# Loading the second weight matrix: plain transfers in SyncE's queue and casts on chip, in place of casting transfers that GpSimd issues

## The chip, the cores and the metric

The kernel runs on one core of a Trainium2 chip. A core has a matrix engine (TensorE, PE), three engines for elementwise work (VectorE or DVE, ScalarE or ACT, GpSimd or POOL) and a sequencer without arithmetic (SyncE, SP). Each runs its own list of instructions in order and waits for the others by semaphores. TensorE reads from the on-chip memory and writes to eight accumulator banks of 128 x 512 float32 values. Transfers between the chip's memory and the core run on 16 DMA engines; an instruction on SP, ACT or POOL issues them.

The metric is the device time of one execution in microseconds, as the median of several runs. Less is better.

## What is computed

A linear attention with decay, followed by a two-layer network with the SiLU function. The attention runs over 4 batches, 8 heads, 768 positions and 64 channels in blocks; its output, 3072 tokens of 512 channels, is the input of the network.

```
# attention, per block of positions (lam: one decay per head)
intra = (qb @ kb^T * Dmask) @ vb
inter = (qb * lam_pow) @ kv_state
out[block] = intra + inter
kv_state = lam_block * kv_state + (kb * rev_pow)^T @ vb

# network on x = attention output as (3072, 512)
h = x @ w_in                       # w_in (512, 2048)
g = h * (1 / (1 + exp(-h)))
y = g @ w_out                      # w_out (2048, 512), y (3072, 512) float32
```

All inputs are float32 in memory. The kernel multiplies in bfloat16 and accumulates in float32.

## The kernel before, in words

**Tiling.** A unit is 128 tokens, and there are 24 of them. Two units make a pair, with its own loads of k, q and v, so there are 12 pairs, numbered from 0; the fifth pair is pair 4. For each pair the kernel casts k and q to bfloat16 (`cast`), scales v by the decay (`scale`), transposes k and q, and multiplies on TensorE. Pairs 0 to 3 are transposed on TensorE, the later ones by a DMA transpose (`dma_turn`, issued by SP). From pair 3 on, the state, score and output matmuls of a pair and of its predecessor are put together as a *burst* (L569 to L622); the masks, state updates and the evacuation into `xt` follow on VectorE, with some of the `xf` updates on GpSimd.

**The network.** `product1` (matmuls at L878, called P1 below) multiplies `xt` by `w_in_bf`: 16 slices of 128 columns of the hidden layer, 4 matmuls each, for two units at a time (256 columns) or four (512). ScalarE applies SiLU and writes the tiles `g`. `product2` (matmuls at L913, called P2) multiplies `g` by `w_out_bf`: 16 matmuls of 512 columns for each unit, one for each slice `ko` of w_out. The result is copied out of the bank (`osb`) and stored by a DMA that ScalarE issues.

**The order.** The program is written as tasks with dependencies, keys and an estimate of their cost on each engine that may run them. A planner (`Planner.order`) runs through them once when the kernel is built, picks at each moment the ready task with the lowest key, and so fixes the order of each engine's instructions and which engine takes a task that several may run. Buffers come from pools with fixed counts: 11 buffers of 512 KB for loads (`raw`), 8 accumulator banks, 36 tiles `g`. Since the order is fixed, a task that is late holds up everything behind it on its engine. The estimates decide the order alone; at run time the semaphores do.

**Loads.** The order of loads follows from a list of words: `u3v` is the v of pair 3, `i0` the first quarter of w_in, `o0` the first quarter of w_out. Loads of q, k, v and w_in are plain transfers in SP's queue. w_in arrives as float32, half a quarter (128 x 2 x 512) in a `raw` buffer, and its 16 pieces of 128 x 512 are cast on GpSimd, ScalarE or VectorE (`copy`, L338 to L342). w_out has another way: four transfers that GpSimd issues write bfloat16 directly into `w_out_bf`, the cast being done by the transfer. They stand behind a *gate*, a copy of one column on GpSimd (L352) that waits for the k of pair 3.

```
sequence = "u0 u1 i0 i1 u2k i2 u2q u2v i3 u3v u3k g3k o0 u3q o1 o2 o3".split()
```

In SP's queue nothing of w_out appears, so the k, q and v of pair 4 follow directly on the q of pair 3. A P2 matmul of slice `ko` waits for quarter `ko // 4` of w_out.

Of the kernel before, what the change touches and what calls it, by code (L numbers as in the profile page):

```python
# [8 lines left out]
F32 = mybir.dt.float32  # L9
# [25 lines left out]
WIDE, CAST, LARGE, PLAIN, TURN = (512, 24.0, 27.0), (256, 14.0, 31.0), (2048, 92.0, 92.0), (2048, 84.0, 84.0), (1024, 46.0, 46.0)  # L35


class Planner:
# [18 lines left out]
    def add(self, key, on, fn, deps=(), bufs=(), nbytes=0, kind=None, prior=(), late=0.0, tag=None):  # L57
        key = key if isinstance(key, tuple) else (key,)
        key = (key[0] + self.SHIFT.get(tag, 0.0),) + key[1:]
        if tag in self.HOME:  # L60
            on = {self.HOME[tag]: on[self.HOME[tag]]}
        t = Task(key, on, fn, deps, list(bufs), nbytes, kind, prior, late)
        t.tag = tag
        for b in t.bufs:
            b.left += 1
            b.pe += "PE" in t.on
        self.tasks.append(t)
        return t
# [163 lines left out]
def kernel(  # L232
# [10 lines left out]
    nc = tc.nc  # L243
# [11 lines left out]
    TIED, SOLO, CROSSED = 3, (3,), range(4, 12)  # L255
    AWAY, XAWAY, OWN = (), (), (0, 1)
    SMALL = (0, 1)
    WKEY, WCAST, WON = -2.0, {"POOL": 0.75, "ACT": 0.62, "DVE": 0.45}, [("POOL", "ACT", "DVE")] * 2 + [("POOL", "DVE"), ("POOL", "ACT")]
    FIRST_ONES, ONES_UNTIL = 10, 19.0

    ctx.enter_context(tc.manual_schedule())
    const = ctx.enter_context(tc.tile_pool(name="const", bufs=1))
# [6 lines left out]
    add = plan.add  # L269
# [4 lines left out]
    def psum_of(b):  # L274
        i = PSUM[b.pool] + b.slot
        return banks[:, i] if b.pool == "bank" else banks[:, i:i + 2]

    def tile_of(b, shape, dt, name):
        if b.tile is None:
            b.tile = psum_of(b) if b.pool in PSUM else sb.tile(shape, dt, tag=f"{b.pool}{b.slot}", name=name)  # L280
        return b.tile
# [3 lines left out]
        out=lam_sb,  # L285
        in_=bass.AP(tensor=lam.tensor, offset=lam.offset, ap=[[0, 128]] + list(lam.ap)),
# [9 lines left out]
        out=ident, in_=ident, compare_op=AL.not_equal, fill=1.0,  # L296
# [10 lines left out]
    for r in halves:  # L307
        nc.gpsimd.affine_select(
            out=tri[r], in_=tri[r], compare_op=AL.is_ge, fill=0.0,
# [22 lines left out]
    w_out_bf = const.tile([128, KO, DM], BF16, name="w_out_bf")  # L332
    w_in_r = moe_w_in.rearrange("(ko p) f -> p ko f", p=128)
    w_out_r = moe_w_out.rearrange("(ko p) f -> p ko f", p=128)

    def copy(e, o, i):
        if e == "ACT":
            nc.scalar.activation(o, i, AF.Copy)  # L338
        elif e == "DVE":
            nc.vector.tensor_copy(o, i)  # L340
        else:
            nc.gpsimd.tensor_copy(o, i)  # L342
# [2 lines left out]
        (nc.vector if e == "DVE" else nc.gpsimd).tensor_tensor(o, a, b, op=AL.mult)  # L345


    gate = const.tile([128, 32], F32, name="gate")

    def gated(key, load, i, tile):  # L350

        t = add(key, {"POOL": 0.15}, lambda e: nc.gpsimd.tensor_copy(gate[:, i:i + 1], tile()), deps=[load],  # L352
                prior=pool_last[-1:])
        pool_last.append(t)

    pool_last = []

    def pool_load(key, w, fn, bufs, nbytes, kind, late=0.0):
        t = add(key, {"POOL": w}, fn, bufs=bufs, nbytes=nbytes, kind=kind, prior=pool_last[-1:], late=late)
        pool_last.append(t)  # L360
        return t

    raw = {}
    LATE, TLATE = 4.0, 4.0

    def parts_of(n):
        return [(0, 1), (2, 3)] if n in FINE else [(0, 1, 2, 3)]
# [21 lines left out]
    wload = {}  # L389

    def load_w(key, what, j):
        if what == "o":
            def go(e):
                nc.gpsimd.dma_start(out=w_out_bf[:, 4 * j:4 * j + 4, :], in_=w_out_r[:, 4 * j:4 * j + 4, :])  # L394

            wload[what, j] = [pool_load((key, 0), 0.8, go, [], 1.0486, LARGE, 0.5)]
            return
        cs = slice(512 * j, 512 * j + 512)
        for h in range(KI // 2):
            b = Buf("raw")  # L400

            def half(e, b=b, h=h):
                nc.sync.dma_start(out=tile_of(b, [128, 2, 512], F32, "raw_w"), in_=w_in_r[:, 2 * h:2 * h + 2, cs])  # L403

            t = add((key, 0, h), {"SP": 0.55}, half, bufs=[b], nbytes=0.5243, kind=PLAIN, late=0.3,
                    tag=("load w", j, h))
            for ko in (2 * h, 2 * h + 1):
                wload[what, j, ko] = add((WKEY + j, ko), {e: WCAST[e] for e in WON[j]},
                                         lambda e, b=b, ko=ko: copy(e, w_in_bf[:, ko, cs], b.tile[:, ko % 2]), deps=[t], bufs=[b],
                                         tag=("cast w", j, ko))  # L410

    sequence = "u0 u1 i0 i1 u2k i2 u2q u2v i3 u3v u3k g3k o0 u3q o1 o2 o3".split() 
    sequence += [f"u{n}" for n in range(NU // 2) if f"u{n}" not in sequence and f"u{n}v" not in sequence]
    for n, x in enumerate(sequence):
        if x[0] == "u":
            which = ["kqv".index(x[-1])] if x[-1] in "kqv" else range(3)
            load_pair(n - 100, int(x[1:].rstrip("kqv")), which)
        elif x[0] == "g":  # L420
            j, i = int(x[1:-1]), "kqv".index(x[-1].lower())
            _, bufs, loads = raw[j]
            g = 0 if x[-1].isupper() else len(parts_of(j)) - 1
            gated((n - 100, -1), loads[i, g], n, lambda buf=bufs[i, g]: buf.tile[:, 0, 0:1])
        else:
            load_w(n - 100, x[0], int(x[1:]))

# [45 lines left out]
    def duo_tile(i):  # L473
        return tile_of(duo_of[i][0], None, F32, "xd")
# [206 lines left out]
    def attention(n):  # L681
# [34 lines left out]
        parts = parts_of(n)  # L716
        xes = [Buf("xs" if n + c in SMALL or n + c in CROSSED else "xe") for c in range(1 if final else 2)]
        xfs = [Buf("xf") for _ in range(0 if final else 2)]
# [89 lines left out]
        for g in range(2):  # L808
# [6 lines left out]
            def inter(e, i=i, g=g, used=used, box=box_x):  # L815
                t = duo_tile(i)
                if n in SMALL:

# [16 lines left out]
            def outputs(e, i=i, g=g, st=st, box=box_x):  # L835
                t = duo_tile(i)
                follow(i)
                for m in range(2):
                    for r in range(2):
# [6 lines left out]
            hold = mask_of[i]  # L846
            im = add((s + g + 0.3, 0, 0), {"PE": 0.056 * 2 * len(used)}, inter, kind="tiled" if n in SMALL else None, bufs=[buf_x, kqT] + [x[0] for _, x in used],
                     deps=hold + cv + turned[min(g, len(turned) - 1)] + [t for _, x in used for t in x[1]], tag=("inter", n, g))
            om = add((s + g + 0.3, 0, 1), {"PE": 0.43 if n in SMALL else 0.28}, outputs, deps=hold + cv + [im], bufs=[buf_x, vd, st], kind="tiled", tag=("outputs", n, g))
            outs[i] = [om]  # L850
# [51 lines left out]
    def product2(u):  # L902
        gi, gp = group_of[u]
        final = u == NU - 1
        cols = [slice(0, 256), slice(256, 512)] if final else [slice(0, 512)]
        for ci, cs in enumerate(cols):
            bank, two = Buf("bank"), Buf("two")
            w = cs.stop - cs.start
            osb = Buf("osb" if w == DM else "osh")

            def mm(e, ko, bank=bank, cs=cs, w=w):
                g, j, _ = gs[gi, ko]
                nc.tensor.matmul(psum_of(bank)[:, :w], lhsT=g.tile[:, j, 128 * gp:128 * gp + 128], rhs=w_out_bf[:, ko, cs],  # L913
                                 start=(ko == 0), stop=(ko == KO - 1))

            prev = None
            s = 4.0 + u + ci * 0.5
            for ko in range(KO):
                g, j, ta = gs[gi, ko]
                prev = add((s + ko / 16, 2), {"PE": w / 2400 + 0.0025}, lambda e, ko=ko, f=mm: f(e, ko),  # L920
                           deps=[ta, prev] + wload["o", ko // 4], bufs=[bank, g, two], kind="p2")

            def evac(e, bank=bank, osb=osb, w=w):
                copy(e, tile_of(osb, [128, w], F32, "osb"), psum_of(bank)[:, :w])

            te = add((s - 1.0, 6), {"DVE": 0.15 + w / 960, "ACT": 0.17 + w / 1200}, evac, deps=[prev], bufs=[bank, osb, two])

            def store(e, cs=cs, osb=osb):
                nc.scalar.dma_start(out=out[128 * u:128 * u + 128, cs], in_=osb.tile)

            add((s - 0.9, 7), {"ACT": 0.1}, store, deps=[te], bufs=[osb], nbytes=0.262 * w / 512, kind=LARGE)

    for n in range(NU // 2):
# [3 lines left out]
                deps=[lam_x] + ready_of[1][3][0], tag="table")  # L937
# [5 lines left out]
    for u in range(NU):  # L943
        product2(u)
# [30 lines left out]
    for start, _, e, t in planned:  # L975
        if e == "PE":
            if not at:
                occupy(vacant(0.5, start), FIRST_ONES, 512)
            elif start < ONES_UNTIL and start - at > 0.15:
                b = vacant(at, start)  # L980
# [34 lines left out]
```

## Time and profile before

| | |
|---|---|
| median of three runs | 212.11 us |
| the runs | 214.0, 212.1, 212.11 us |
| the profiled execution | 213.39 us |
| its span, first to last instruction | 211.7 us |
| granted TensorE clock | 0.998 |
| bytes read and written | 27.27 MB read, 6.29 MB written |

The busy time of the engines and the rate of the transfers, by stretches of the span:

| stretch, us | PE | DVE | ACT | POOL | GB/s moved |
|---|---|---|---|---|---|
| 20 to 30 | 9.91 | 7.87 | 7.69 | 3.51 | 355 |
| 30 to 40 | 10.00 | 7.31 | 7.80 | 3.92 | 249 |
| 40 to 50 | 9.81 | 7.29 | 7.02 | 0.61 | 217 |
| 50 to 60 | 9.09 | 1.56 | 5.24 | 0.00 | 206 |
| 60 to 70 | 9.95 | 6.09 | 6.01 | 2.37 | 338 |

TensorE's busy time counts overlapping matmuls as one stretch, and the modelled end of a matmul lies behind the start of the next. A row such as "x26" with a start and a length is a run of equal matmuls; the pace is read from the starts of the rows that follow each other. A few matmul records are missing from the trace (572 and 383 rows where 576 and 400 were issued).

The four casting transfers are issued from 33.8 to 36.9 us. The k and q of pair 5, issued by SP at 35.35 and 36.82, land 19.7 us later; the loads ahead of them took 6 to 9 us.

### The profile page before, as it was taken

Reading aid. Unit: us, or ns where it says so; the run is one execution under the profiler, and the core shown is the slowest. Engines: PE = TensorE matmul, PEld = TensorE weight load, DVE = VectorE, ACT = ScalarE, POOL = GpSimd, SP = SyncE. Lnnn points to the kernel's source line nnn. Section 1 sums busy time; section 2 is a strip of 40 time slices with the busy share of each in tenths; the row PEclk is TensorE's granted clock in tenths of the full one; section 3 lists DMA queues with packets and bytes.
Section 4 is the critical chain, followed back from the end, with each engine's and each line's share of the span. In section 5 each row is a group of like instructions: output and inputs, shape, how many; then the busy total and the mean of one; then the engine's idle time right before and its main releaser. Section 6 shows DMA issues by size and latency. Waiting matters only on the chain.

```text
span 211.7 us, 5407 instructions
## 1 busy us (share of the span) xinstructions
PE 202.5 (96%) x2343; PEld 122.6 (58%) x2364; DVE 104.5 (49%) x181; ACT 113.6 (54%) x166; POOL 22.7 (11%) x38
## 2 busy tenths in 40 slices
PE   7998999998999999999999999999999999999993
PEld 2776878865656567676864545454444444444452
DVE  3897878672038758595859696645201110111000
ACT  3687877782566457765756452735444444444121
POOL 4027426010002100010400001300000000000000
PEclk9999999999999999999999999999999999999999
DMA  4999999999999999999999340101011101110212
GB/s 118 336 379 366 365 327 286 188 217 234 184 303 333 320 266 291 123 315 226 254 266 225 92 130 0 54 3 50 0 53 50 50 0 50 53 50 0 99 53 95
DMA packets 62183, 36.00 MB, mean 170 GB/s; under 512 B 18000, under 2 KB 57168, under 8 KB 62160
## 3 DMA queue, kind: packets, MB, share of 16 engines
q1 hardware_dynamic: 56304, 27.27, 51.2%
q10 hardware_dynamic: 3744, 6.30, 8.1%
q0 software_dynamic: 2112, 2.10, 6.0%
q8 instruction: 18, 0.29, 0.6%
q14 instruction: 5, 0.04, 0.1%
HBM read 27.27 MB, written 6.29 MB: 159 GB/s over the span
## 4 chain that ended last, share of the span: by engine, by line
PE 70%; DMA 15%; SPq 7%; DVE 3%; issue 2%; POOL 1%; ACT 0%; DVEq 0%
PE banks L913 35%; PE banks L878 28%; DMA w_out_bf<-in_moe_w_out_dram 8%; SPq L378 4%; DMA raw<-in_k_dram 4%; DMA raw_w<-in_moe_w_in_dram 4%; SPq L403 3%; PE banks L578 2%; PE banks L622 2%; PE banks L585 1%; DVE st L345 1%; PE banks L611 1%; POOL w_out_bf L394 1%; DVE xs_all L345 1%; DVE kq L340 1%
## 5 line engine op out<-in xcount | busy, mean ns | idle before, releaser
L878 PE MATMUL banks<-xt,w_in_bf 128*128 128x256 bf16 (+1 forms) x572 | 113.3, 308 | 0.7 <-POOL w_in_bf L342 0.5
L913 PE MATMUL banks<-w_out_bf,g 128*128 128x512 bf16 (+1 forms) x383 | 107.1, 370 | 2.7 <-issue 1.3
L894 ACT ACTIVATE g<-banks 128x512 bf16<-128x512 f32 x96 | 70.3, 744 | 55.7 <-PE banks L878 51.7
L878 PEld LDWEIGHTS <-w_in_bf 128*128 128x128 bf16 x576 | 55.3, 98 | 30.3 <-POOL w_in_bf L342 0.9
L913 PEld LDWEIGHTS <-g 128*128 128x128 bf16 x400 | 38.5, 98 | 41.7 <-issue 1.0
L345 DVE TENSOR_TENSOR st<-banks,tri 128x512 bf16<-128x512 f32 (+1 forms) x42 | 29.6, 759 | 6.1 <-PE banks L622 5.0
L340 DVE COPY osb<-banks 128x512 f32<-128x512 f32 x8 | 5.5, 692 | 49.8 <-PE banks L913 49.8
L345 DVE TENSOR_TENSOR xt<-banks,lam_xe 128x512 bf16<-128x512 f32 x24 | 15.7, 687 | 24.1 <-PE banks L578 23.2
L338 ACT ACTIVATE osb<-banks 128x512 f32<-128x512 f32 (+1 forms) x17 | 9.7, 570 | 28.7 <-PE banks L913 28.7
L338 ACT ACTIVATE kq<-raw 64x512 bf16<-64x512 f32 (+2 forms) x29 | 22.7, 812 | 3.5 <-ACT osb L338 1.7
L345 POOL TENSOR_TENSOR xf<-y,lam_be 128x256 f32<-128x256 f32 (+1 forms) x13 | 11.9, 914 | 104.0 <-DVE y L740 104.0
L345 DVE TENSOR_TENSOR vd<-raw,lam_v 128x1024 bf16<-128x1024 f32 (+1 forms) x13 | 14.8, 1138 | 2.9 <-DMA raw<-in_v_dram 2.8
L340 DVE CAST kq<-raw 64x512 bf16<-64x512 f32 (+3 forms) x29 | 14.1, 518 | 3.3 <-DMA raw<-in_k_dram 2.5
L950 PE MATMUL banks<-ones 128*128 128x128 bf16 (+1 forms) x88 | 10.3, 266 | 1.5 <-DVE ones L291 1.5
L345 DVE TENSOR_TENSOR xs_all<-y,lam_be 64x256 bf16<-64x256 f32 (+2 forms) x21 | 9.6, 460 | 0.4
L622 PE MATMUL banks<-kqT 64*64 64x128 bf16 x288 | 9.5, 217 | 0.0
L950 PEld LDWEIGHTS <-ones 128*128 128x128 bf16 x88 | 5.9, 103 | 4.0 <-issue 2.2
L622 PEld LDWEIGHTS <-kqT 64*64 64x64 bf16 x288 | 7.4, 107 | 0.0
L740 DVE TENSOR_TENSOR y<-banks,xf 128x256 f32<-128x256 f32 (+1 forms) x17 | 6.7, 401 | 1.0 <-POOL xf L345 1.0
L611 PE MATMUL banks<-vd,kq 64*64 64x64 bf16 x240 | 6.9, 194 | 0.0
L338 ACT ACTIVATE kqT<-banks 128x512 bf16<-128x512 bf16 (+1 forms) x6 | 4.9, 810 | 2.4 <-PE banks L530 2.4
L342 POOL CAST w_in_bf<-raw_w 128x512 bf16<-128x512 f32 x8 | 5.5, 684 | 6.2 <-DMA raw_w<-in_moe_w_in_dram 6.1
(49 smaller groups left out, 73.3 us busy)
## 6 DMA issues: line engine op xcount, KB each, us to landing
out_dram<-osb ACTq DMA_DIRECT2D x23, 256.0 KB, 2.0
raw<-in_k_dram SPq DMA_DIRECT2D x11, 512.0 KB, 6.1
raw<-in_q_dram SPq DMA_DIRECT2D x11, 512.0 KB, 6.3
raw<-in_v_dram SPq DMA_DIRECT2D x11, 512.0 KB, 7.4
raw_w<-in_moe_w_in_dram SPq DMA_DIRECT2D x8, 512.0 KB, 7.9
w_out_bf<-in_moe_w_out_dram POOLq DMA_DIRECT2D x4, 512.0 KB, 14.0
raw<-in_k_dram SPq DMA_DIRECT2D x2, 256.0 KB, 4.8
raw<-in_q_dram SPq DMA_DIRECT2D x2, 256.0 KB, 5.3
```

What stands on the lines that cost most here:

```text
L338: nc.scalar.activation(o, i, AF.Copy)
L340: nc.vector.tensor_copy(o, i)
L345: (nc.vector if e == "DVE" else nc.gpsimd).tensor_tensor(o, a, b, op=AL.mult)
L378: nc.sync.dma_start(out=tile_of(bufs[i, g], [128, 2 * len(ms), 128], F32, "raw"), in_=src[i][heads(ms)].rearrange("h (p r) d -> p h (r d)" ...
L403: nc.sync.dma_start(out=tile_of(b, [128, 2, 512], F32, "raw_w"), in_=w_in_r[:, 2 * h:2 * h + 2, cs])
L611: mm = nc.tensor.matmul(psum_of(db)[d, 256 * c + 64 * k:256 * c + 64 * k + 64], lhsT=kq_of()[halves[c], 0, r, 2 * k + (h ^ c if n in CROSS ...
L622: nc.tensor.matmul(t[c, k % 2, r, :], lhsT=t_of()[halves[row], 0, r, k, c], rhs=t_of()[halves[row], 1, :, k, c], start=(k % 2 == 0 and r = ...
L740: nc.vector.tensor_tensor(tile_of(src, [128, NP, 64], F32, "y")[:, sl], d_of(), old[0].tile[:, sl], op=AL.add)
L878: nc.tensor.matmul(t[:, j, :], lhsT=w_in_bf[:, ko, 128 * m:128 * m + 128], rhs=xt[gi].tile[:, ko, :], start=(ko == 0), stop=(ko == KI - 1))
L894: nc.scalar.activation(t, psum_of(bank).rearrange("p (jc r a) -> p jc r a", r=2, a=64), AF.Silu)
L913: nc.tensor.matmul(psum_of(bank)[:, :w], lhsT=g.tile[:, j, 128 * gp:128 * gp + 128], rhs=w_out_bf[:, ko, cs], start=(ko == 0), stop=(ko == ...
L950: nc.tensor.matmul((t if b.pool == "bank" else t[:, 0])[:, 0:w], lhsT=ones[:, 0:128], rhs=ones[:, 0:w], start=True, stop=True)
```

## The change

- The four casting transfers, the gate and the chain that keeps GpSimd's issues in order are gone.
- `load_w` treats w_out as w_in: each quarter comes in two halves of 128 x 2 x 512 float32, plain transfers in SP's queue into `raw` buffers, and each half gives two pieces of 128 x 512 that are cast into `w_out_bf`. Any of GpSimd, ScalarE and VectorE may take a piece. The casts have the key `OKEY + 0.5 * j`.
- In the list of loads, two quarters (four halves) follow the q of pair 3, then come the k, q and v of pair 4, then the other two quarters.
- A P2 matmul of slice `ko` waits for the cast of piece `ko` alone.

The same bytes are read from memory. The planner is unchanged but gets other tasks, so the order of instructions changes on all engines from the q of pair 3 on.

```diff
+    OKEY = 0.0
...
-    gate = const.tile([128, 32], F32, name="gate")
-
-    def gated(key, load, i, tile):
-
-        t = add(key, {"POOL": 0.15}, lambda e: nc.gpsimd.tensor_copy(gate[:, i:i + 1], tile()), deps=[load],
-                prior=pool_last[-1:])
-        pool_last.append(t)
-
-    pool_last = []
-
-    def pool_load(key, w, fn, bufs, nbytes, kind, late=0.0):
-        t = add(key, {"POOL": w}, fn, bufs=bufs, nbytes=nbytes, kind=kind, prior=pool_last[-1:], late=late)
-        pool_last.append(t)
-        return t
...
     def load_w(key, what, j):
-        if what == "o":
-            def go(e):
-                nc.gpsimd.dma_start(out=w_out_bf[:, 4 * j:4 * j + 4, :], in_=w_out_r[:, 4 * j:4 * j + 4, :])
-
-            wload[what, j] = [pool_load((key, 0), 0.8, go, [], 1.0486, LARGE, 0.5)]
-            return
         cs = slice(512 * j, 512 * j + 512)
         for h in range(KI // 2):
             b = Buf("raw")
 
             def half(e, b=b, h=h):
-                nc.sync.dma_start(out=tile_of(b, [128, 2, 512], F32, "raw_w"), in_=w_in_r[:, 2 * h:2 * h + 2, cs])
+                nc.sync.dma_start(out=tile_of(b, [128, 2, 512], F32, "raw_w"), in_=w_in_r[:, 2 * h:2 * h + 2, cs] if what == "i"
+                                  else w_out_r[:, 4 * j + 2 * h:4 * j + 2 * h + 2, :])
 
             t = add((key, 0, h), {"SP": 0.55}, half, bufs=[b], nbytes=0.5243, kind=PLAIN, late=0.3,
-                    tag=("load w", j, h))
+                    tag=("load w" if what == "i" else "load o", j, h))
             for ko in (2 * h, 2 * h + 1):
+                if what == "o":
+                    wload[what, 4 * j + ko] = add((OKEY + 0.5 * j, ko), WCAST,
+                                                  lambda e, b=b, ko=ko: copy(e, w_out_bf[:, 4 * j + ko, :], b.tile[:, ko % 2]), deps=[t],
+                                                  bufs=[b], tag=("cast o", j, ko))
+                    continue
...
-    sequence = "u0 u1 i0 i1 u2k i2 u2q u2v i3 u3v u3k g3k o0 u3q o1 o2 o3".split() 
+    sequence = "u0 u1 i0 i1 u2k i2 u2q u2v i3 u3v u3k u3q o0 o1 u4 o2 o3".split() 
...
-                           deps=[ta, prev] + wload["o", ko // 4], bufs=[bank, g, two], kind="p2")
+                           deps=[ta, prev, wload["o", ko]], bufs=[bank, g, two], kind="p2")
```

More of the change, by code (lines that the diff above doesn't have):

```diff
@@ L419 @@
             load_pair(n - 100, int(x[1:].rstrip("kqv")), which)
[L420 to L424, printed above, removed]
         else:
```

## The prediction

> **What bounds the kernel now.** I read the page, then the chain of waits in order of time, the timelines of the engines around w_out, and the durations of the casts that w_in already gets on chip. First the page: busy time and share of the 211.7 us span by engine, and the chain's shares.
>
> ```profile
> PE 202.5 (96%) x2343; PEld 122.6 (58%) x2364; DVE 104.5 (49%) x181; ACT 113.6 (54%) x166; POOL 22.7 (11%) x38
> ...
> PE 70%; DMA 15%; SPq 7%; DVE 3%; issue 2%; POOL 1%; ACT 0%; DVEq 0%
> ```
>
> TensorE (PE) is the bound; there is little idle time to win. Where it waits, the chain in order of time (start, length) tells:
>
> ```profile
> 33.63 0.19 POOL gate L352
> 33.81 1.62 POOL w_out_bf L394 x2
> 35.44 16.02 DMA w_out_bf<-in_moe_w_out_dram
> 51.46 0.04 issue
> 51.50 0.81 PE banks L913 x3
> ```
>
> The casting transfers of w_out end a wait of PE at 51.50; behind it the chain is almost all PE to the end. PE's timeline shows the wait's size:
>
> ```profile
> 37.15 1.91 PE L878 MATMUL banks<-xt,w_in_bf 128*128 128x256 bf16 x16
> ...
> 39.96 3.01 PE L878 MATMUL banks<-xt,w_in_bf 128*128 128x256 bf16 x26
> 43.06 1.90 PE L913 MATMUL banks<-w_out_bf,g 128*128 128x512 bf16 x7
> ...
> 48.52 2.13 PE L878 MATMUL banks<-xt,w_in_bf 128*128 128x256 bf16 x18
> 51.50 0.81 PE L913 MATMUL banks<-w_out_bf,g 128*128 128x512 bf16 x3 [0.86 <-DMA w_out_bf<-in_moe_w_out_dram]
> ```
>
> A first-product matmul (P1, L878, 256 columns) takes 0.108 us in a full stretch (29 in 3.17 us from 78.27), a second-product one (P2, L913, 512 columns) 0.216 (12 in 2.59 from 70.31). So 18 P1 from 48.52 end at 50.46 and the next P2 comes 1.04 later. And 26 P1 from 39.96 end at 42.77, yet the first P2 comes at 43.06, 0.29 later. That fits the first quarter of w_out: the first issue is at 33.75, and the shortest landing is 9.3 us:
>
> ```profile
> DMA to landing us min/median/max: 9.3/14.0/18.7
> ```
>
> w_out thus costs PE about 1.04 + 0.29 = 1.3 us, and that is the whole prize: after it PE has no wait worth naming.
>
> **The change, part by part.** *Removed:* the gate and four issues on GpSimd (0.19 and 3.18 us). GpSimd is then idle for 6.5 us: worth nothing by themselves.
>
> *Added casts.* Sixteen pieces of 128x512: the built order gives GpSimd 6, ScalarE 5, VectorE 5. The same casts of w_in are in the trace:
>
> ```profile
> L342 POOL CAST w_in_bf<-raw_w x8: 611/650/822, 16.4 to 30.6; 128x512 bf16<-128x512 f32 x8
> L338 ACT ACTIVATE w_in_bf<-raw_w x6: 611/631/631, 15.9 to 30.5; 128x512 bf16<-128x512 f32 x6
> L340 DVE CAST w_in_bf<-raw_w x2: 417/628/839, 24.0 to 24.3; 128x512 bf16<-128x512 f32 x2
> ```
>
> GpSimd 6 x 0.65 = 3.9 us, ScalarE 5 x 0.63 = 3.2, VectorE 5 x 0.42 to 0.84 = 2.1 to 4.2. Cover between 36 and 54 us: GpSimd is idle but for one 0.61 us multiply at 43.39; ScalarE waits 1.21 + 0.60 + 1.86 + 2.23 = 5.9 us for PE; VectorE waits 1.72 + 0.81 + 1.83 us and then sits idle from 50.2 to 58.6. The busy time is hidden; what counts is when each piece is ready.
>
> *When the pieces land.* SP's order becomes: third input of pair 3 (q), four halves of w_out, k, q, v of pair 4, four halves, pair 5. The anchor is that q, which lands as ScalarE's cast of it starts; the pace of halves shows in GpSimd's timeline, where two casts each start on a landing, 1.42 us apart:
>
> ```profile
> 35.23 1.06 ACT L338 ACTIVATE kq<-raw 128x1024 bf16<-128x1024 f32 x1 [0.40 <-DMA raw<-in_q_dram]
> ```
> ```profile
> 18.45 0.68 POOL L342 CAST w_in_bf<-raw_w 128x512 bf16<-128x512 f32 x1 [0.61 <-DMA raw_w<-in_moe_w_in_dram]
> 19.10 0.61 POOL L345 TENSOR_TENSOR xf<-y,lam_be 128x256 f32<-128x256 f32 x1
> 19.87 0.61 POOL L342 CAST w_in_bf<-raw_w 128x512 bf16<-128x512 f32 x1 [0.15 <-DMA raw_w<-in_moe_w_in_dram]
> ```
>
> Loads of q, k, v come 1.6 us apart (k of pair 3 at 33.57, q at 35.2). So halves 0 to 3 land at 36.6, 38.0, 39.4, 40.8; pair 4 at 42.4, 44.0, 45.6; halves 4 to 7 at 47.0, 48.4, 49.8, 51.2. No buffer holds SP up: the eleven input buffers that these loads take are freed by casts done by 36.3.
>
> *When PE asks for them.* The built order is the same up to the row at 37.15, of which 10 of 16 P1 stay: end 38.23. Then 6 P2; pieces 2 and 3 (half 1: 38.0 + 0.65 = 38.7) are asked for at 38.9. Six P2 end at 39.5; the burst of pair 3 (0.97 us, from 38.99 in the trace) ends at 40.5; 24 P1 and 9 P2 with it end at 45.0; the next burst (0.96: 44.80 to 45.76) ends at E = 46.0. Then one P2 and 18 P1: piece 8 is asked for at E + 2.15 = 48.2, and half 4 plus a cast is 47.7. Piece 10 at E + 3.45 = 49.5 (half 5: 49.1), piece 12 at E + 4.75 = 50.8 (50.5), piece 14 at E + 6.36 = 52.4 (half 7: 51.9). All are in time, by 0.2 to 0.5 us.
>
> *Queues passed.* VectorE runs in order, and pieces 8, 10 and 12 stand between its xt work (1.3 us after the burst) and pair 4's casts (0.76 us each): ends at E + 1.8, E + 3.0, E + 4.2 with casts of 0.42; E + 2.2, E + 3.9, E + 5.5 with 0.84. Against E + 2.15, 3.45, 4.75 that is a wait of 0 or of 0.75; I take 0.2, nearer to the short one, since GpSimd's casts rarely run at that moment. On ScalarE the pieces stand before silus of P1 still in one of several banks: nothing.
>
> *Moved loads.* Pair 4's k and q come 5.6 us later; its transpose waits for VectorE's last cast of it, E + 3.8 = 49.8 (46.20 now). Behind pair 5's k and q (52.8, 54.4) it lands at 56.3 by the 1.9 us between the landings of q and transpose now (56.52, 58.41), or 62.0 by the longest landing, 12.2 us. Its burst comes 87 P1 and 39 P2 after E: 46.0 + 17.8 = 63.8. Covered by 2 to 7 us. Later bursts come 2.2 us earlier to 2.7 later in the order, and the least lead of a transpose now is 4 us (issued at 81.41, landed 12.0 later, for the burst at 97.36).
>
> *Sum:* -1.3 + 0.2 = -1.1 us. The profiled run is 213.39 us (span 211.7 and 1.69 around it), so 212.3; the median of the three runs is 212.11, 1.28 below it, so **211.0**.
>
> [...] The trace's VectorE casts took 417 and 839 ns, the long one beside a GpSimd cast that took 0.80. [...]
>
> **The rivals.**
> *No gain (chance 0.22): 212.1, within 0.5.* The transfers are at their limit anyway: from 35.2 to 51.5 three loads and eight halves' worth of w_out land, 11 x 0.524 MB in 16.3 us, 354 GB/s; I have the same eleven landing by 51.2. Only the order of landing against PE's order makes a gain, and slacks of 0.2 to 0.5 us can be lost: a wait at piece 2, 8 or 14 of about 1 us takes the old one's place. Against it: the last half is asked for at 52.4 where now the wait ends at 51.5 with 10 more P2 still to come before piece 15. [...]
> *Slower (0.20): the pace.* If the eleven transfers land p us apart, half 7 is cast at 35.2 + 11p + 0.65, against 52.4. My pace is 1.45; a wait begins at p = 1.51, and slower by 1% (2.1 us net) at 1.82. At p = 1.9: 56.75, 4.35 late, less 1.3: +3.1, 215.2. For it: k and q of pair 5 landed 19.7 us after issue, and the moved bytes fell to 217 GB/s from 40 to 50 us. Against: both sat beside the casting transfers; ahead of them the pace was 1.4 to 1.6.
> *Faster by over 1% (0.05).* It needs 2.1 us; PE has 1.3, and the rest would have to come out of the 1.69 us around the span, if a queue of GpSimd's is set up there. Bounds 0 and 1.69 (209.1); no row shows any of it, so 0.
>
> **Numbers.** Forecast 0.53. A measurement here tells about 1% from no change: 210.0 to 214.2. The forecast and the first rival lie within: 0.53 + 0.22 = 0.75 same; 0.20 slower by the pace, 0.05 faster. PE's order after the wait held without idle time in the trace, which is why the forecast has the most; slacks this small, why it has no more. Range 210.2 (whole prize, some of the surround) to 214.8 (p near 1.87).
>
> **What would show it.** Right: no wait of PE on w_out at 51.5, the first L913 near 38.2, the transpose of pair 4 landing before 62, PE's busy share up half a point. Wrong: a new wait ahead of L913 between 38 and 53 released by a cast (my slack was lost) or with GpSimd's casts waiting for raw_w landings over 1.8 us apart (the pace).

## The result and the profile after

| | before | after |
|---|---|---|
| median of six runs each, us | 212.12 | 215.54 |
| lowest to highest, us | 212.1 to 214.0 | 215.17 to 215.7 |
| the profiled execution, us | 213.39 | 215.7 |
| its span, us | 211.7 | 213.7 |
| round the span (time less span), us | 1.69 | 2.0 |

The kernel became slower: the ratio is 1.0137, with an interval of 1.0103 to 1.0172, so less than 2% but clear of the noise. The forecast was 211.0, with a range that ended at 214.8. Against before, +3.42 us came where -1.1 was forecast.

The page of the kernel after: span, busy time of the engines, and the shares of the chain of waits.

```profile
span 213.7 us, 5445 instructions
...
PE 204.7 (96%) x2364; PEld 122.5 (57%) x2364; DVE 109.8 (51%) x188; ACT 115.5 (54%) x169; POOL 22.6 (11%) x39
...
PE 75%; DMA 12%; SPq 8%; DVE 2%; ACT 1%; issue 1%; POOL 1%
```

TensorE's share is the same 96%, and the chain still has 20% of transfers and their issue (22% before). The shares do not say where 3.4 us went. TensorE's timeline does. Up to the loads of w_out the order of the instructions is the same on TensorE, yet the first P1 of the program starts a microsecond later; the first transfer of w_out is issued only after 32 us. First before, then after:

```profile
17.20 2.07 PE L878 MATMUL banks<-xt,w_in_bf 128*128 128x256 bf16 x15 [0.45 <-POOL w_in_bf L342]
```
```profile
18.20 0.61 PE L858 MATMUL banks<-xt,w_in_bf 128*128 128x256 bf16 x4
19.56 1.37 PE L858 MATMUL banks<-xt,w_in_bf 128*128 128x256 bf16 x11 [0.74 <-DVE st L346]
```

Going back further, VectorE's first casts wait for the first loads. In brackets stand the idle time and what ended it. Before, the first q of the program has landed at 6.01 us; after, the cast of it starts at 6.39, and a later one waits again at 9.04.

```profile
6.01 0.43 DVE L340 CAST kq<-raw 128x512 bf16<-128x512 f32 x1 [0.30 <-DMA raw<-in_q_dram]
```
```profile
6.39 0.43 DVE L341 CAST kq<-raw 128x512 bf16<-128x512 f32 x1 [0.45 <-DMA raw<-in_q_dram]
...
9.04 0.43 DVE L341 CAST kq<-raw 128x512 bf16<-128x512 f32 x1 [0.21 <-DMA raw<-in_q_dram]
```

So the same transfers, issued by the same instructions, move more slowly. The window from 5 to 15 us shows it (start:end, length, busy us of PE, PEld, DVE, ACT and POOL with counts, granted clock, DMA share, GB/s). Before, then after: 352 GB/s against 304, at the same clock of 1.00 and at a DMA share that is no lower. The DMA engines are as occupied, and move less.

```profile
5.00:15.00 10.00, 9.42 (x196) 7.29 (x198) 8.46 (x18) 7.23 (x15) 0.29 (x1) 1.00 1.11 352
```
```profile
5.00:15.00 10.00, 8.21 (x176) 6.42 (x175) 7.52 (x15) 6.19 (x14) 0.00 (x0) 1.00 1.15 304
```

The lateness grows up to the end of w_out's loads. The q of pair 3, put at 35.2 by the forecast, ends ScalarE's wait at 37.49:

```profile
37.49 1.06 ACT L339 ACTIVATE kq<-raw 128x1024 bf16<-128x1024 f32 x1 [0.20 <-DMA raw<-in_q_dram]
```

TensorE after, around w_out. The first P2 is at 40.69 (forecast 38.23). The old wait at 51.5 is gone: the P2 at 51.03 names none. New ones have come, 0.16 us ahead of piece 2 and 0.54 us at the last half:

```profile
40.69 0.81 PE L893 MATMUL banks<-w_out_bf,g 128*128 128x512 bf16 x3
41.66 0.81 PE L893 MATMUL banks<-w_out_bf,g 128*128 128x512 bf16 x3 [0.16 <-POOL w_out_bf L343]
...
51.03 1.03 PE L893 MATMUL banks<-w_out_bf,g 128*128 128x512 bf16 x4
...
56.08 1.02 PE L893 MATMUL banks<-w_out_bf,g 128*128 128x512 bf16 x4 [0.54 <-POOL w_out_bf L343]
```

The chain of waits of the kernel after (start, length, what ran) says the same: the last half of w_out lands at 46.83 + 8.54 = 55.37, GpSimd casts it, and TensorE goes on.

```profile
46.83 8.54 DMA raw_w<-in_moe_w_out_dram
55.42 0.62 POOL w_out_bf L343
56.08 1.02 PE banks L893 x4
```

From the landing of the q at 37.46 to 55.37 eleven transfers landed, on average 1.63 us apart. The forecast had 1.45. The pace is not even: the first ten are 1.53 apart, and the last half comes 2.57 behind the one ahead of it, at 52.80. The waits for casts of w_out are 0.70 us together; most of the 3.4 us was lost ahead of them.

What slows a transfer whose instruction is unchanged? One deleted line of the diff reaches every buffer: `gate`, a tile of 128 x 32 float32, takes 128 bytes of each partition of the on-chip memory and lay ahead of the load buffers. In the built program before, the first load buffer starts at byte 60672 of a partition, which is 237 x 256. After, it starts at 60544, which is 128 over a multiple of 256. All load buffers move with it, and with them every tile that is allocated behind `gate`. Single packets fit that. A load of q, k or v writes packets of 512 bytes, one of w_in packets of 2 KB; their times are read from the packet records of the two traces:

```
                     512-byte packets issued 5 to 14 us, ns     2 KB packets, 12 to 30 us, ns
                     5% / median / 95% / mean                   median / mean
before               27 / 27 / 27 / 27.2                        84 / 88.1
after                27 / 32 / 38 / 31.7                        87 / 91.0
```

### The profile page after: what moved, and what is told of

It reads as the page before. It is cut to its first block, busy times and chain, and to the rows that moved or that the text cites. A ratio compares the mean times of both kernels' runs of the same rounds, so it can differ in the third digit from the quotient of the medians.

```text
span 213.7 us, 5445 instructions
## 1 busy us (share of the span) xinstructions
PE 204.7 (96%) x2364; PEld 122.5 (57%) x2364; DVE 109.8 (51%) x188; ACT 115.5 (54%) x169; POOL 22.6 (11%) x39
## 3 DMA queue, kind: packets, MB, share of 16 engines
q1 hardware_dynamic: 58480, 31.46, 58.2%
## 4 chain that ended last, share of the span: by engine, by line
PE 75%; DMA 12%; SPq 8%; DVE 2%; ACT 1%; issue 1%; POOL 1%
PE banks L893 37%; PE banks L858 31%; DMA raw_w<-in_moe_w_out_dram 7%; DMA raw<-in_q_dram 5%; SPq L364 4%; SPq L383 4%; PE banks L602 2%; PE banks L558 2%; PE banks L565 1%; DVE st L346 1%; PE banks L591 1%; POOL w_out_bf L343 1%; ACT g L874 0%; DVE kq L341 0%; PE banks L510 0%
## 5 line engine op out<-in xcount | busy, mean ns | idle before, releaser
L858 PE MATMUL banks<-xt,w_in_bf 128*128 128x256 bf16 (+1 forms) x576 | 116.1, 308 | 0.9 <-DVE st L346 0.7
L893 PE MATMUL banks<-w_out_bf,g 128*128 128x512 bf16 (+1 forms) x400 | 113.3, 371 | 0.7 <-POOL w_out_bf L343 0.7
L341 DVE COPY osb<-banks 128x512 f32<-128x512 f32 x13 | 9.0, 692 | 57.0 <-PE banks L893 51.7
L339 ACT ACTIVATE kq<-raw 64x512 bf16<-64x512 f32 (+2 forms) x32 | 24.0, 780 | 4.1 <-DMA raw<-in_k_dram 1.7
L346 POOL TENSOR_TENSOR xf<-y,lam_be 128x256 f32<-128x256 f32 (+1 forms) x13 | 11.0, 848 | 89.3 <-DVE y L720 89.3
L341 DVE CAST kq<-raw 64x512 bf16<-64x512 f32 (+3 forms) x26 | 13.4, 534 | 5.6 <-DMA raw<-in_k_dram 2.7
L339 ACT ACTIVATE osb<-banks 128x512 f32<-128x512 f32 (+1 forms) x12 | 6.7, 561 | 16.5 <-PE banks L893 16.5
L930 PE MATMUL banks<-ones 128*128 128x128 bf16 (+1 forms) x88 | 9.7, 259 | 1.5 <-DVE ones L292 1.5
L346 DVE TENSOR_TENSOR xs_all<-y,lam_be 64x256 bf16<-64x256 f32 (+2 forms) x21 | 10.4, 497 | 0.4
L510 PE MATMUL banks<-ident,kq 128*128 128x128 bf16 x64 | 5.3, 220 | 1.9 <-DVE kq L341 1.4
```

The lines of the kernel that those rows point to most:

```text
L858: nc.tensor.matmul(t[:, j, :], lhsT=w_in_bf[:, ko, 128 * m:128 * m + 128], rhs=xt[gi].tile[:, ko, :], start=(ko == 0), stop=(ko == KI - 1))
L930: nc.tensor.matmul((t if b.pool == "bank" else t[:, 0])[:, 0:w], lhsT=ones[:, 0:128], rhs=ones[:, 0:w], start=True, stop=True)
```

## The experiments

The main theory was that the new address of the load buffers costs the time. Its rivals were the new transfers and casts themselves, and, for the part outside the span, that GpSimd no longer issues a transfer. They ran in three series, each beside before: its median was 212.51 us for the first four rows, 212.5 for the next four and 212.35 for the last. In every row, "address" is what the start of the load buffers is over a multiple of 256 bytes. The ratio, with its 95% interval, is not the quotient of the two medians.

| kernel | address | median, us | runs | ratio to before, interval |
|---|---|---|---|---|
| after_pad128 | 0 | 212.81 | 10 | 1.0016, 0.9989 to 1.0043 |
| after_pad256 | 128 | 215.85 | 4 | 1.0157, 1.0133 to 1.0182 |
| before_shift128 | 128 | 215.86 | 4 | 1.016, 1.0137 to 1.0184 |
| before_wout256 | 0 | 212.33 | 10 | 0.9985, 0.9965 to 1.0005 |
| after_loads_only | 0 | 212.71 | 10 | 1.003, 1.0 to 1.0061 |
| after_pad64 | 192 | 215.66 | 4 | 1.0163, 1.0137 to 1.0189 |
| after_pad384 | 0 | 213.04 | 10 | 1.0028, 1.0009 to 1.0046 |
| after_pad128_pool | 0 | 213.14 | 10 | 1.0025, 1.0002 to 1.0048 |
| before_without_wout | 0 | 212.21 | 12 | 0.9989, 0.996 to 1.0018 |

With the address given back the changed kernel is equal to before or slightly slower: the four intervals reach from 0.9989 to 1.0061, and for after_pad384 and after_pad128_pool they lie just above 1.

### The 128 bytes given back, and twice as many

The kernel after with an unused tile where `gate` was. For after_pad256 it is 64 wide.

```diff
+    pad = const.tile([128, 32], F32, name="pad")
     raw = {}
```

> The changed kernel with an unused tile of 128 bytes per partition where the gate tile stood; nothing else differs, so every load buffer has its address of before again (a multiple of 256 bytes; in the changed kernel 128 over). Theory A, the addresses: the loss sits in the first 30 us, where both kernels issue the same loads and the changed one lands them later; with the old addresses the 512-byte packets take 27 ns again, the first P1 starts near 17.2 us and the time is about 211.0 to 212 us (the prediction's sum). Rival B, the queue: the loss comes with the absence of GpSimd's DMA queue or with the casts, and addresses do not matter: 215.5 us again, first P1 near 18.2.

> The changed kernel with an unused tile of 256 bytes per partition: an added tile, but the load buffers stay 128 bytes off a multiple of 256. Theory A: 215.5 us, as the changed kernel. If any shift or any added tile helped, it would fall to 212. Rival B: 215.5.

An unused tile takes the loss away, and a larger one brings it back: 215.85 - 212.81 = 3.04 us, with the same instructions in both kernels. The page of after_pad128: its span, the DMA queue of the loads (packets, MB, share of 16 engines' time; 58.2% in the kernel after for the same packets and bytes), and the chain, in which transfers have 7% instead of 12.

```profile
span 210.5 us, 5422 instructions
...
q1 hardware_dynamic: 58480, 31.46, 53.5%
...
PE 86%; DMA 7%; ACT 2%; issue 2%; DVE 1%; POOL 1%; SPq 0%
```

The window from 5 to 15 us of after_pad128 moves 341 GB/s, near the 352 of before:

```profile
5.00:15.00 10.00, 9.71 (x192) 7.62 (x194) 8.37 (x18) 7.20 (x15) 0.23 (x1) 1.00 1.10 341
```

TensorE of after_pad128. Against the same rows of after (18.20, 40.69, 56.08) it is ahead by 0.95, then 2.19, then 3.16 us, and it names a wait on w_out only once, 0.23 us:

```profile
17.25 2.03 PE L859 MATMUL banks<-xt,w_in_bf 128*128 128x256 bf16 x15 [0.44 <-POOL w_in_bf L343]
...
38.50 0.60 PE L894 MATMUL banks<-w_out_bf,g 128*128 128x512 bf16 x2
39.32 0.81 PE L894 MATMUL banks<-w_out_bf,g 128*128 128x512 bf16 x3 [0.23 <-POOL w_out_bf L343]
...
52.92 1.03 PE L894 MATMUL banks<-w_out_bf,g 128*128 128x512 bf16 x4
```

### The same shift in the kernel before

before_shift128 has only a wider `gate`. before_wout256 has that, and a tile of 128 bytes ahead of `w_out_bf`, which lies 128 over a multiple of 256 in both kernels: with both edits `w_out_bf` and the load buffers start on multiples of 256. Both kernels have this edit:

```diff
-    gate = const.tile([128, 32], F32, name="gate")
+    gate = const.tile([128, 64], F32, name="gate")
```

And before_wout256 alone:

```diff
+    pad = const.tile([128, 32], F32, name="pad")
     w_out_bf = const.tile(
```

> The kernel before with a gate tile of 256 bytes per partition in place of 128: all transfers as before, the load buffers 128 bytes off a multiple of 256. Theory A: the first P1 starts near 18.2 us and the time goes up by 2 to 4 us, to 214 to 216. Rival B: 212.1.

> The kernel before with the tile that the casting transfers write, w_out_bf, moved to a multiple of 256 bytes (it lies 128 over in both kernels); the load buffers keep their alignment. Theory A in its wide form, any transfer is slowed by such an address: the casting transfers land earlier than 51.5 us and the 1.0 us wait for them shrinks, time 211.2 to 212. In its narrow form, only 512-byte packets are slowed, and rival B: 212.1.

Without any of the change's transfers or casts, the shift alone costs 215.86 - 212.51 = 3.35 us. In its trace the casting transfers start later too, and TensorE waits 1.22 us for the first quarter of w_out; how much of the 3.35 us this makes is not shown. TensorE's first P1 in before_shift128 starts where it does after, at 18.21:

```profile
18.21 0.61 PE L878 MATMUL banks<-xt,w_in_bf 128*128 128x256 bf16 x4 [0.21 <-POOL w_in_bf L342]
```

The address of `w_out_bf`, which the casting transfers write, made no difference that shows: 0.9985, and the interval holds 1.

### Loads alone, and other distances

In after_loads_only the load buffers have a pool of their own behind 128 bytes; the other tiles stay 128 bytes over a multiple of 256, as they are after, though most of them move. after_pad64 and after_pad384 are after_pad128 with a pad of 16 and of 96 columns.

```diff
+    ld = ctx.enter_context(tc.tile_pool(name="ld", bufs=1))
...
-            b.tile = psum_of(b) if b.pool in PSUM else sb.tile(shape, dt, tag=f"{b.pool}{b.slot}", name=name)
+            b.tile = psum_of(b) if b.pool in PSUM else (ld if b.pool in ("raw", "rawh") else sb).tile(shape, dt, tag=f"{b.pool}{b.slot}", name=name)
...
+    pad = ld.tile([128, 32], F32, name="pad")
```

> The changed kernel with its load buffers in a region of their own that begins with an unused 128-byte tile: the load buffers lie at multiples of 256 bytes, all other buffers (bfloat16 copies, transposed tiles, output tiles) stay 128 bytes over. Theory A1: the loads alone lose by the address; time as with the 128-byte tile, 212.3 to 213.0 us, 512-byte packets in 27 ns. Theory A2: stores, transposes or the engines lose too; then between 213 and 215.5.

> The changed kernel with an unused tile of 64 bytes: load buffers 192 bytes over a multiple of 256. If what costs is that a 512-byte packet does not begin at a multiple of 256, then as at 128: 215 to 216 us, the first P1 near 18.2. If the cost grows with the piece that is cut off at either end, or multiples of 64 suffice, it differs: up to 1.5 us less.

> The changed kernel with an unused tile of 384 bytes: load buffers at multiples of 512 (with the 128-byte tile: multiples of 256 that are 256 over a multiple of 512). If 256 is all that counts: 212.3 to 213.0, as with the 128-byte tile. If packets of 512 bytes gain from a start at a multiple of 512: below 212.3, packets under 27 ns.

The load buffers suffice: with all other tiles 128 bytes over, as after, the time is 212.71 and the first P1 is back:

```profile
17.18 2.08 PE L860 MATMUL banks<-xt,w_in_bf 128*128 128x256 bf16 x15 [0.43 <-POOL w_in_bf L344]
```

192 over costs what 128 over does (215.66, first P1 at 18.45), and a pad of 384 bytes is as good as one of 128 (213.04 and 212.81, intervals that overlap). The packets of all these kernels, in the columns of above:

```
                     address   512-byte packets, ns       2 KB packets, ns
after_pad128           0       27 / 27 / 27 / 27.3        84 / 87.6
after_loads_only       0       27 / 27 / 27 / 27.5        84 / 86.2
after_pad384           0       27 / 27 / 27 / 27.4        84 / 86.6
after_pad256         128       27 / 32 / 38 / 31.5        88 / 91.0
before_shift128      128       27 / 32 / 38 / 31.8        88 / 90.9
after_pad64          192       27 / 33 / 40 / 32.5        88 / 91.2
```

A load of 512 KB in 512-byte packets is 1024 packets, 64 for each of 16 engines: 4.5 ns more for each is 0.29 us. Pairs 0 to 4 make 15 such loads, 4.3 us, and the 16 halves of w_in and w_out some 0.05 each. If the engines had never been idle, the last half of w_out would have come 5.1 us later. It came 3.5 later (55.37 against 51.85 in after_pad128).

### The time round the span

Round the span the kernel before and its variants spend 1.65 to 1.78 us, after and its variants 1.93 to 2.05. One theory was that this 0.26 us comes of GpSimd issuing no transfer. after_pad128_pool is after_pad128 with one small transfer of GpSimd's into the pad:

```diff
+    nc.gpsimd.dma_start(out=pad[:, 0:8], in_=w_out_r[:, 0, 0:8])
```

> The changed kernel with the 128-byte tile, and one small transfer (128 x 32 bytes of w_out into that tile, which nobody reads) issued by GpSimd ahead of the first task. Theory C: the 0.25 us more outside the span (1.94 to 2.02 us in the changed kernel and its variants, 1.65 to 1.77 in the kernel before and its variants) come with a program in which GpSimd issues no transfer; then 1.65 to 1.77 again and a time of 212.5. If they have another source: 1.94 to 2.02 and 212.8.

That theory fell: 2.09 to 2.15 us, not 1.7. What the 0.26 us is stays open.

### What the prize was

before_without_wout leaves the load of w_out out and fills `w_out_bf` with zeros on GpSimd in its place, so that no P2 can wait for a transfer of it. The other two are single profiled executions of the kernel before, unchanged.

```diff
-                nc.gpsimd.dma_start(out=w_out_bf[:, 4 * j:4 * j + 4, :], in_=w_out_r[:, 4 * j:4 * j + 4, :])
+                nc.gpsimd.memset(w_out_bf[:, 4 * j:4 * j + 4, :], 0.0)
```

> The kernel before without the load of w_out: in place of each casting transfer GpSimd fills the same quarter of the bfloat16 tile with zeros (so the product is zero; all instructions of TensorE stay and wait for the fills, and 4.2 MB less are read). It bounds what any change of w_out's loading can win. Theory D1: the 1.04 us wait of the profiled execution is absent in the typical one (spans of the kernel before lie at 210.4 in half of the executions and at 211.2 to 212.1 in a third), so the whole prize is about 0.3 us in the median: 212.0 to 212.4. Theory D2, the prediction's: 1.3 us are lost to w_out in every execution; then 211.0 to 211.3.

> The kernel before once more, unchanged, for its trace alone. Theory D1: if its span is near 210.4, PE has no wait for w_out near 50 us; if it is near 211.7, it has one of about 1 us. Theory D2: the wait is there whatever the span.

> The same, a second trace of the kernel before. Theory D1: span and wait go together, 210.4 without and 211.7 with it. Theory D2: the wait is there whatever the span.

Without any transfer of w_out the kernel takes 212.21 us, beside 212.35 for before in the same series: 0.14 us, with an interval that holds 1. The two executions show why. In the first (213.89 us, span 212.2) TensorE waits 1.58 us, and at the first quarter of w_out, not mainly at the third as in the profile that the prediction shows:

```profile
44.55 1.90 PE L913 MATMUL banks<-w_out_bf,g 128*128 128x512 bf16 x8 [1.58 <-DMA w_out_bf<-in_moe_w_out_dram]
```

In the second (212.23 us, span 210.5) it waits at neither place:

```profile
42.89 1.89 PE L913 MATMUL banks<-w_out_bf,g 128*128 128x512 bf16 x8
...
50.30 0.81 PE L913 MATMUL banks<-w_out_bf,g 128*128 128x512 bf16 x3
```

So the wait belongs to single executions. Of the 16 runs of before in that series, 12 have spans of 210.4 to 211.1 us, and four of 211.5 to 212.5. The profiled run of the prediction, with 211.7, is of the second kind. That all four lie there because of w_out isn't shown: one of the 12 runs without its transfers also has a span of 212.8.

## Why the prediction was wrong

**The step that failed.** "Removed: the gate and four issues on GpSimd ... worth nothing by themselves." The gate was costed as an instruction, 0.19 us of an idle engine. As a tile it held the load buffers on a multiple of 256 bytes, and without it the kernel loses 3.04 us. No row of the trace of before could price that, but the addresses of the built programs could have been compared. Against before, forecast and result are 4.5 us apart (-1.1 and +3.42). With the address given back +0.30 is left, so about 3.1 of the 4.5 us are the address, 1.1 the gain that did not come, and 0.3 what is left, nearly all of it round the span.

**What hung on it.** "The built order is the same up to the row at 37.15" is true of the order and false of the times: the first P1 is 1.00 late, the q of pair 3 lands at 37.46 instead of 35.2, the pace is 1.63 instead of 1.45.

**The slower rival.** It named the place where the wait came, the last half of w_out, and its threshold of 1.51 us was passed. Its price was not right: 35.2 + 11 x 1.63 + 0.65 = 53.8 would be 1.4 us late, about what the prize was to give. The rest of the loss lies ahead of it, in the q that is 2.26 late, which the rival kept in place. Its cause was another, too: it looked for a slower pace in what the casting transfers had shown, and the pace slowed by the address, from the first load on.

**The prize.** "-1.3" was read from one execution, and then the whole difference of 1.28 between that execution and the median was taken off again. The median run hardly has the wait: without w_out's transfers it gains 0.14. So most of that microsecond was counted twice. Even with the address given back the kernel takes 212.81, not 211.0.

**Round the span.** Taken as 0, with bounds that held only a gain. It is a loss of 0.26 us, nearly all that after_pad128 is above before: 212.81 - 212.51 = 0.30, within the interval of no change.

**The landings and the cover**, with the address given back, came out near the forecast. GpSimd's timeline in after_pad128 shows the cast of half 1, which ended at 39.27 where 38.7 was forecast, and of half 7:

```profile
38.40 0.87 POOL L343 CAST w_out_bf<-raw_w 128x512 bf16<-128x512 f32 x1 [0.66 <-DMA raw_w<-in_moe_w_out_dram]
...
51.89 0.89 POOL L343 CAST w_out_bf<-raw_w 128x512 bf16<-128x512 f32 x1 [3.04 <-DMA raw_w<-in_moe_w_out_dram]
```

From the q at 35.81 to half 7 at 51.85 the pace is 1.46, as forecast; but that is a mean of 1.39 for the first ten steps and 2.12 for the last, and its agreement with 1.45 is partly luck. What makes the last step long, here and in the kernel after, is open. The first P2 is at 38.50 (38.23), the last pieces are asked for at 52.92 (52.4). The transpose of pair 4 is issued at 50.87 and lands at 57.6 (forecast 49.8 and 56.3), and its burst comes at 64.52 (63.8), so the later loads are hidden by 6.9 us.

**The lateness of 0.2** had the right size and the wrong engine: 0.23 us, at piece 2 and behind GpSimd, not at pieces 8 to 12 behind VectorE. The casts of w_out in after_pad128 by engine (count; minimum, median and maximum ns; first and last start):

```profile
L343 POOL CAST w_out_bf<-raw_w x6: 609/613/889, 37.1 to 51.9; 128x512 bf16<-128x512 f32 x6
...
L341 DVE CAST w_out_bf<-raw_w x5: 419/427/428, 38.4 to 50.7; 128x512 bf16<-128x512 f32 x5
```

Here VectorE's pieces all had the short time, and GpSimd took a long one, 0.87 us from 38.40, beside a VectorE cast that had begun at 38.37. (Its other long one, 0.89 from 51.89, ran beside VectorE's scaling of v, which lasted from 51.09 to 52.31.) In the kernel after it is the other way round for one piece: GpSimd's cast began first and kept 0.62 us, and VectorE's took 0.72:

```profile
38.37 0.43 DVE L341 CAST w_out_bf<-raw_w 128x512 bf16<-128x512 f32 x1
```
```profile
51.51 0.62 POOL L343 CAST w_out_bf<-raw_w 128x512 bf16<-128x512 f32 x1 [0.47 <-DMA raw_w<-in_moe_w_out_dram]
51.69 0.72 DVE L341 CAST w_out_bf<-raw_w 128x512 bf16<-128x512 f32 x1
```

In these rows the cast that starts second takes the longer time. So it was in the trace of before: VectorE's long cast began at 24.32, behind a GpSimd cast from 24.05 (which took 0.82 us, not the 0.80 that the prediction gives). Why it does, these rows do not show.

**The other rivals.** "No gain" is what the transfers and casts are worth by themselves: 1.0016, with 1 in the interval. Its number held with the address given back, its mechanism did not: no wait of about 1 us took the old one's place, since the median run had little of the old one to lose. "Faster" didn't come.

## What to carry to other kernels

A tile that is deleted or resized moves every tile behind it in its pool: compare the start addresses of the load buffers in the two built programs, and keep them on a multiple of 256 bytes when packets are as short as 512 (against after_pad128, distances of 128 and 192 cost 3.04 and 2.85 us here; no other was run). A wait in one profiled execution is a prize only as far as the other runs have it; compare its span with theirs before subtracting it, and do not take off the distance to the median as well. When the same instructions run later from the very start, look at the bytes and the time of single packets before looking at what was added.

## What the runs showed of the hardware

- In these runs a load whose buffer starts 128 or 192 bytes over a multiple of 256 is dear: the mean 512-byte packet issued from 5 to 14 us takes 31.5 to 32.5 ns instead of 27.2 to 27.5, spread over 27 to 38 or 40 (5% to 95%) where nearly all took 27; 2 KB packets take 87 to 88 (median) instead of 84. With the load buffers on a multiple of 256, the medians of the three layouts of the kernel after that were run lie within 0.33 us (212.71 to 213.04).
- When a VectorE cast and a GpSimd cast overlapped, the one that started second took longer: GpSimd 0.87 us instead of 0.61 behind a VectorE cast begun 0.03 us earlier, VectorE 0.72 instead of 0.43 behind a GpSimd cast begun 0.18 us earlier.
- By distance, the mean 512-byte packet takes 31.5 to 31.8 ns at 128 over and 32.5 ns at 192 over, against 27.2 to 27.5 on a multiple of 256: some 16 and 19% more. Pads of 128 and 384 bytes are alike, at 27.3 and 27.4 ns. What happens to a packet on the way is not shown by these runs.
- The time round the span differs by 0.26 us between two kernels with the same inputs and outputs, and went up, not down, to 2.09 to 2.15 when GpSimd got one small transfer.
